# Six difference pieces of w_out: made in DRAM by an accumulating transfer, or on VectorE

## The chip, the core and the metric

The kernel runs on one core of one Trainium2 chip. The core has engines that each work through a queue of their own in order: TensorE (PE; its weight loads are shown as PEld), VectorE (DVE), ScalarE (ACT), GpSimd (POOL) and SyncE (SP), which issues the transfers of this kernel. The metric is the time of one execution on the device in microseconds (us).

## The reference

A gated linear attention runs over the sequence, and a feed-forward layer with squared ReLU follows. With batch 4, 8 heads, 768 steps and head size 48:

```python
for t in range(S):
    state = alpha[:, :, t, :, None] * state + np.einsum('bhd,bhe->bhde', k[:, :, t], v[:, :, t])
    y[:, :, t] = np.einsum('bhd,bhde->bhe', q[:, :, t], state)
x = y.transpose(0, 2, 1, 3).reshape(B * S, H * D)     # 3072 x 384
h = np.maximum(x @ w_in, 0.0)                         # w_in 384 x 2048
out = h * h @ w_out                                   # w_out 2048 x 384
```

All arrays are float32.

## The kernel before

The tokens are worked in 6 groups (`NG`) of 4 blocks (`GB`) of 128 tokens. For each group there are attention steps (states of blocks of 128 steps) and the two layers of the feed-forward part, `layer_in` (x times w_in) and `layer_out` (times w_out). The order of all work is written out by hand: a group's feed-forward steps are a list of `units`, each with a cost, and `weave` puts `events` (attention steps, loads, the preparation of weights) between them where the sum of the costs reaches the event's time. The events' times are numbers in the table `AT`; they are not microseconds. Each engine then runs its instructions in that order.

Group 0 and the first part of `layer_out` of groups 0 and 1 multiply in plain float32. Otherwise each float32 matrix is cut into two matrices of TensorE's faster type float32r, a high part and a rest, and a product is made of three passes. For weights, piece p of 8 (128 x 768 numbers, 384 KB) of layer w ("i" or "o") is prepared by four steps, `wstep` apart (`prepare`, line 580):

- `cast_w` (line 549): ScalarE writes the high part b, the tile `wb`. It stays in SBUF.
- `rest_w` (559): VectorE writes l = w - b, the tile `wl`.
- `scale_w` (563): ScalarE scales l by 1/E, and `keep` (555) has SP store it to DRAM.
- `diff_w` (568): VectorE writes d = b - l, the tile `wd`, and `keep` has SP store that, too.

VectorE's operations of these steps go through `combine` (line 545) and so all show line 547. Activations (x, h) are cut by `split_to` (595) and `diff_to` (599) in the same way.

The parts in DRAM are called `kept_parts`; in the profile `li`, `di`, `lo`, `do` are the l and d parts of w_in and w_out. `pump` (585) loads them back into `wl` and `wd` in the order of the list `todo`, when the part has been stored and the count of tiles in use allows it (`room`); `used` calls it when a part has been read for the last time in a group. All weights' tiles come from one pool of 26, `wt`. `stream` puts the parts of the next group on the list.

Of w_out, pieces 6 and 7 are prepared during group 0 (`o0`). Pieces 4, 5, 0, 1, 2, 3 are prepared during group 1, at the times 23, 26, 29, 35, 42, 36 (`o2`); `diff_w` stands 4.8 later. In group 1 the passes of `layer_out` (line 701, by `out_x` and `out_y`) read the parts of pieces 4 to 7, and pieces 0 to 3 are multiplied plainly by `out_plain`. The l parts of pieces 4 to 7 and the d parts of 6 and 7 stay in SBUF after their preparation; the d parts of pieces 0 to 5 don't, and are loaded from DRAM when they are wanted.

The attention of a pair of blocks is made of `turn` (transposes on TensorE of q and k, line 482, after the products of line 284 on VectorE), `ga` and `gb`. Between `ga` and `gb` a no-op on GpSimd hands over from matmuls of the one to those of the other:

```python
            passed = nc.gpsimd.nop(nofuse=True)
            dep(passed, end)
```

It waits for the last matmul of `ga`, and the first of `gb` waits for it. GpSimd has no other work after the kernel's first microseconds.

## Time and profile before

| what | value |
|---|---|
| median of 3 runs | 522.79 us (522.51 to 523.1) |
| span of the profiled execution | 520.6 us |
| PE busy | 510.8 us, 98% of the span |
| VectorE busy | 366.0 us, 70% |
| ScalarE busy | 313.0 us, 60% |
| GpSimd busy | 5.4 us, 1% |
| transfers | 102.36 MB, a mean of 197 GB/s; 68.3% of the 16 DMA engines' span |
| granted TensorE clock | 1.00 |

The profiled execution's own time is its span, from the first to the last instruction; the runs' times also hold what lies around the span, 2.2 us at the median. A line of a group in the profile reads: line, engine, operation, output<-inputs, shapes, count, then busy us, mean ns of one, and the idle time of the engine before them with what ended it. SPq is SP's queue of transfers. The stage in which the six pieces are prepared lies between about 165 and 205 us.

### The profile page before, as it was taken

How to read it: one execution, taken by the hardware profiler on the slowest of the kernel's cores; microseconds unless marked ns; L12 is line 12 of the kernel's file. 1: busy time of each engine (PE TensorE's matmuls, PEld its weight loads, DVE VectorE, ACT ScalarE, POOL GpSimd, SP SyncE). 2: the span in 40 equal slices, each digit the busy share in tenths (PEclk: the TensorE clock that was granted, in tenths of full speed). 3: DMA queues.
4: the chain of work that ended last, by engine and by line, in shares of the span. 5: the costliest groups of instructions: out<-in, count | busy, mean ns of one | idle time of the engine just before them, and what ended most of it. 6: DMA issues, size and time to landing. Idle time of an engine off the chain costs nothing.

```text
span 520.6 us, 12925 instructions
## 1 busy us (share of the span) xinstructions
PE 510.8 (98%) x5276; PEld 418.2 (80%) x5276; DVE 366.0 (70%) x631; ACT 313.0 (60%) x650; POOL 5.4 (1%) x29
## 2 busy tenths in 40 slices
PE   7989999999999999999999999999999999999997
PEld 4754455668887668988899988899988899988997
DVE  4798989979978787867597476587465476363861
ACT  4668785677888594575963275963275763164620
POOL 4000000000000000000000000000000000000000
PEclk9999999999999999999999999999999999999999
DMA  9999687244686787898884788964673534898201
GB/s 161 209 278 213 196 240 218 60 114 176 224 200 196 195 246 198 264 317 206 195 248 148 251 246 198 230 187 150 231 255 126 179 126 151 268 340 293 70 0 62
DMA packets 140995, 102.36 MB, mean 197 GB/s; under 512 B 111476, under 2 KB 114568, under 8 KB 140936
## 3 DMA queue, kind: packets, MB, share of 16 engines
q1 hardware_dynamic: 140936, 101.53, 68.3%
q8 instruction: 42, 0.69, 0.6%
q14 instruction: 17, 0.14, 0.1%
HBM read 84.18 MB, written 17.33 MB: 195 GB/s over the span
## 4 chain that ended last, share of the span: by engine, by line
PE 93%; DVE 2%; SPq 2%; DMA 1%; issue 1%; POOL 1%; ACT 0%; POOLq 0%; DVEq 0%
PE o L701 41%; PE h L622 32%; PE h L805 7%; PE y L352 4%; PE T L482 2%; PE sckv L372 2%; PE sckv L395 2%; PE cs L265 1%; DMA qk_lent<-in_q_dram 1%; SPq L303 1%; SPq L109 1%; PE cs L268 1%; PE cs L269 1%; DVE x L515 0%; DVE w_in L182 0%
## 5 line engine op out<-in xcount | busy, mean ns | idle before, releaser
L622 PE MATMUL h<-xa,wb 128*128 128x512 f32 x240 | 68.2, 392 | 0.0
L622 PE MATMUL h<-xl,wl 128*128 128x512 f32 x240 | 67.9, 391 | 0.0
L622 PE MATMUL h<-xd,wd 128*128 128x512 f32 x240 | 67.3, 396 | 0.0
L515 ACT COPY x<-y 32x256 f32<-32x256 f32 (+2 forms) x132 | 47.2, 366 | 25.4 <-PE y L352 20.1
L547 DVE TENSOR_TENSOR hid<-h,hid 128x512 f32<-128x512 f32 x40 | 27.6, 689 | 45.5 <-PE h L622 45.4
L701 PE MATMUL o<-wb,ha 128*128 128x384 f32 x160 | 54.6, 342 | 0.0
L701 PE MATMUL o<-w_out,hid 128*128 128x384 f32 x160 | 54.0, 491 | 0.0
L701 PE MATMUL o<-wd,hd 128*128 128x384 f32 x304 | 53.8, 334 | 0.0
L701 PE MATMUL o<-wl,hl 128*128 128x384 f32 x160 | 53.5, 335 | 0.0
L639 ACT ACTIVATE h<-h 128x512 f32<-128x512 f32 x40 | 23.3, 582 | 49.7 <-PE h L622 49.7
L622 PEld LDWEIGHTS h<-xl,wl 128*128 128x128 f32 x240 | 45.1, 188 | 10.0 <-DVE xl L547 0.4
L701 PEld LDWEIGHTS o<-wd,hd 128*128 128x128 f32 x304 | 52.7, 188 | 0.3 <-DVE osb L737 0.3
L622 PEld LDWEIGHTS h<-xa,wb 128*128 128x128 f32 x240 | 44.6, 188 | 9.3 <-ACT xa L596 0.2
L622 PEld LDWEIGHTS h<-xd,wd 128*128 128x128 f32 x240 | 44.2, 188 | 9.2
L701 PE MATMUL o<-wb,hx 128*128 128x384 f32 x144 | 48.7, 338 | 0.0
L701 PE MATMUL o<-wl,hx 128*128 128x384 f32 x144 | 48.1, 334 | 0.0
L701 PEld LDWEIGHTS o<-w_out,hid 128*128 128x128 f32 x160 | 29.8, 190 | 19.3
L637 ACT ACTIVATE hid<-h 128x512 f32<-128x512 f32 x40 | 24.0, 600 | 34.6 <-PE h L622 34.5
L805 PE MATMUL h<-x,w_in 128*128 128x512 f32 (+1 forms) x108 | 43.6, 552 | 1.2 <-ACT x L515 1.2
L596 ACT ACTIVATE ha<-hid 128x512 fp32r<-128x512 f32 x40 | 25.6, 639 | 25.5 <-DVE hx L547 16.1
L805 PEld LDWEIGHTS h<-x,w_in 128*128 128x128 f32 x108 | 19.9, 190 | 21.1 <-issue 17.2
L547 DVE TENSOR_TENSOR hl<-hid,ha 128x512 fp32r<-128x512 f32 x40 | 27.5, 688 | 10.1 <-ACT ha L596 10.1
(114 smaller groups left out, 879.7 us busy)
## 6 DMA issues: line engine op xcount, KB each, us to landing
wd<-do SPq DMA_DIRECT2D x36, 384.0 KB, 3.7
wl<-lo SPq DMA_DIRECT2D x34, 384.0 KB, 4.0
wl<-li SPq DMA_DIRECT2D x32, 384.0 KB, 3.5
wd<-di SPq DMA_DIRECT2D x32, 384.0 KB, 3.9
raw<-in_moe_w_in_dram SPq DMA_DIRECT2D x8, 768.0 KB, 5.6
raw<-in_moe_w_out_dram SPq DMA_DIRECT2D x8, 768.0 KB, 5.6
v_in<-in_v_dram SPq DMA_DIRECT2D x24, 192.0 KB, 4.7
out_dram<-osb SPq DMA_DIRECT2D x24, 192.0 KB, 1.9
```

Of the source, the lines that this page charges most:

```text
L352: ins = nc.tensor.matmul(out=ys[e][64 * half : 64 * half + D + G * e, m % 2, p // 2, t], lhsT=lhsT, rhs=rhs, start=(half, e) not in seen, ...
L372: nc.tensor.matmul(out=ps[e][HALF[h], 0, p, :], lhsT=ks[rows, p, HALF[h]], rhs=qs[rows, p, HALF[h]], start=True, stop=True, skip_group_che ...
L395: nc.tensor.matmul(out=ps[h][64 * e : 64 * (e + 1), 1, p, G:64], lhsT=tile_of("k", n)[HALF[h], 2 * p + e, :], rhs=tiles["v"][n % NV][HALF[ ...
L482: nc.tensor.transpose(out=ps[h][:, i, p, :], in_=rows[HALF[h], 128 * p : 128 * (p + 1)], identity=ident[HALF[h], HALF[h]],)
L515: copy(out=x[kk][to : to + m, t : t + 2], in_=blk[n]["y"][e][r : r + m, :, p // 2],)
L547: nc.vector.tensor_tensor(out=o, in0=x, in1=z, op=op)
L596: nc.scalar.activation(out=a, in_=x, func=AF.Copy, scale=NEAR)
L622: nc.tensor.matmul(out=acc["h", j], lhsT=here[w, "i", p][:, kk, jj * 128 : (jj + 1) * 128], rhs=x_parts[x][:, kk], start=start and kk == 0 ...
L637: nc.scalar.activation(out=hid[j], in_=x, func=AF.Copy, scale=E)
L639: nc.scalar.activation(out=x, in_=x, func=AF.Copy, scale=1.0 + E)
L701: nc.tensor.matmul(out=acc[t][:, 0:DM], lhsT=lhs[:, t * C : (t + 1) * C], rhs=rhs, start=start, stop=stop, skip_group_check=True,)
L805: nc.tensor.matmul(out=ps, lhsT=w[:, kk, c0 : c0 + 128], rhs=xT[g][kk][:, cols], start=(kk == 0), stop=(kk == KM - 1),)
```

## The change

For w_out's pieces 0 to 5 VectorE no longer makes d. `cast_w` has SP store the high part b at the place in DRAM where d is to be, and `diff_w` has GpSimd issue a transfer that adds the scaled rest l from SBUF to what lies there. So that an addition serves, the rest is scaled by -1/E instead of 1/E; the signs in `split_to` and `diff_to` are turned as well, so that the products of two rests are unchanged. For the other pieces VectorE adds instead of subtracting.

```diff
+    def summed(w, p):
+        return w == "o" and p < NW - AT["k0"]
+
     def cast_w(w, p):
         b = here["b", w, p] = wt("wb", FP32R, shapes[w])
         nc.scalar.activation(out=b, in_=whole[w][p], func=AF.Copy, scale=NEAR)
+        if summed(w, p):
+            nc.sync.dma_start(out=kept_parts["d", w, p], in_=words(b))
...
     def scale_w(w, p):
         l = made["l", w, p]
-        nc.scalar.activation(out=l, in_=l.bitcast(FP32), func=AF.Copy, scale=1.0 / E)
+        nc.scalar.activation(out=l, in_=l.bitcast(FP32), func=AF.Copy, scale=-1.0 / E)
         keep("l", w, p)
 
     def diff_w(w, p):
         b, l = here["b", w, p].bitcast(FP32), made["l", w, p].bitcast(FP32)
-        d = made["d", w, p] = wt("wd", FP32R, shapes[w])
         cut.add((w, p))
-        combine(((d, b, ALU.subtract, l),))
-        keep("d", w, p)
+        if summed(w, p):
+            nc.gpsimd.dma_start(out=kept_parts["d", w, p], in_=words(l), accum_op=ALU.add)
+            stored.add(("d", w, p))
+        else:
+            d = made["d", w, p] = wt("wd", FP32R, shapes[w])
+            combine(((d, b, ALU.add, l),))
+            keep("d", w, p)
         for x in "ld":
+            if x == "d" and summed(w, p):
+                continue
             t = made.pop((x, w, p))
...
     def split_to(a, l, x):
         nc.scalar.activation(out=a, in_=x, func=AF.Copy, scale=NEAR)
-        combine(((l, x, ALU.subtract, a.bitcast(FP32)),))
+        combine(((l, a.bitcast(FP32), ALU.subtract, x),))
 
     def diff_to(d, a, l):
         nc.vector.scalar_tensor_tensor(
-            out=d, in0=a.bitcast(FP32), scalar=-E, in1=l.bitcast(FP32), op0=ALU.mult, op1=ALU.add
+            out=d, in0=a.bitcast(FP32), scalar=-E, in1=l.bitcast(FP32), op0=ALU.mult, op1=ALU.subtract
         )
```

## The prediction

> **What bounds the kernel now.** I read the page's busy row and chain first, then the windows of the stage in which the six pieces are prepared, then the waits and timelines of that stage. In this text a piece is named by its number in w_out; the six are prepared in the order 4, 5, 0, 1, 3, 2, and their accumulating transfers are called A4, A5, A0, A1, A3, A2.

> ```profile
> PE 510.8 (98%) x5276; PEld 418.2 (80%) x5276; DVE 366.0 (70%) x631; ACT 313.0 (60%) x650; POOL 5.4 (1%) x29
> PE 93%; DVE 2%; SPq 2%; DMA 1%; issue 1%; POOL 1%; ACT 0%; POOLq 0%; DVEq 0%
> 166.00:217.00 51.00, 50.04 (x742) 39.38 (x741) 40.85 (x73) 33.03 (x76) 0.00 (x0) 1.00 0.76 210
> ```

> The first line is the busy time of each engine, the second the chain that ended last, the third the window 166 to 217 us (PE, PEld, DVE, ACT, POOL busy; granted clock; DMA share; GB/s). TensorE is busy for 50.04 of 51 us at full clock and makes the chain. VectorE is busy for 40.85, so it has 10 us to spare. The waits of this window and the timelines of PE, VectorE, ScalarE and SP give the few places where another engine comes close:

> ```profile
> PE y L352 <- issue: 1.0, 1, 1.0
> PEld T L482 <- DVE q_in L284: 0.5, 1, 0.5
> DVE wl L547 <- DMA do<-wd: 0.2, 1, 0.2
> ```
> ```profile
> 181.32 0.84 ACT L565 ACTIVATE wl<-wl 128x768 fp32r<-128x768 f32 x1
> ...
> 189.41 0.96 DVE L547 TENSOR_TENSOR wl<-w_out,wb 128x768 fp32r<-128x768 f32 x1 [0.19 <-DMA do<-wd]
> ...
> 191.89 0.96 DVE L547 TENSOR_TENSOR wd<-wb,wl 128x768 fp32r<-128x768 f32 x1
> 192.76 0.55 DVE L284 TENSOR_TENSOR q_in<-q_in,b 128x384 f32<-128x384 f32 x1
> ...
> 194.97 0.46 PE L482 MATMUL T<-ident,k_in 64*128 64x64 f32 x8
> 204.05 0.33 PE L352 MATMUL y<-am,v_in 64*48 64x64 f32 x3 [0.96 <-issue]
> 211.75 5.71 PE L701 MATMUL o<-wd,hd 128*128 128x384 f32 x32
> ```

> In the second fence the columns are start, duration, engine, line, operation. TensorE's only idle time in the stage is the 0.96 us before 204.05, which no engine ends. No wait of TensorE's matmuls is put down to a `wd` operation.

> **Removed.** Six VectorE subtractions of one 128x768 piece:

> ```profile
> L547 DVE TENSOR_TENSOR wd<-wb,wl 128x768 fp32r<-128x768 f32 x6 | 5.7, 954 | 0.4 <-PE o L701 0.4
> ```

> That is 6 x 0.954 = 5.7 us of VectorE, all beside TensorE's matmuls. The bound of the gain is TensorE's idle time in the stage, 0.96 us; I take 0, since that gap has no releaser on VectorE. The six stores of d behind `diff_w` go, too.

> **Added on SP.** Six stores of the high part, as many bytes as the six that go, but issued at `cast_w`. SP is in order, so each holds the queue until ScalarE's cast ends. Piece 4's cast ends at 165.8 and the `row` stores behind it, at 163.7 before, come some 2.5 us later; the `last` loads that read those rows are issued at 169.6, after loads that wait for the transposes of 167.7, and VectorE uses them first at 176.9. Covered. The stores of pieces 1 and 3 wait for casts that end near 188.4 and push two a_in loads from 187.5 to about 188.9; these belong to the next stage, which begins at 217. Covered. Without the cover a held SP costs its holding time.

> **Added on POOL.** Six accumulating transfers. POOL's queue else carries in this stage only the two hand-offs of line 456, at 176.86 and 204.42, for which TensorE waits at 179.52 and 207.31. In program order A4 stands before the first; A0, A1 and A3 before the second. A4 can start at 169.6 (end of its scaling), A3 at 193.0, so POOL's own time for issuing one would have to pass 9.9 us, or some 14 us, before TensorE waits. The trace has no transfer issued by POOL; an issue by SP is 0.32 to 0.47 us here. Cost 0.

> **The accumulate's duration, T.** No row shows one. [...] The nearest rows:

> ```profile
> wd<-do SPq DMA_DIRECT2D x36, 384.0 KB, 3.7
> ...
> lo<-wl SPq DMA_DIRECT2D x8, 384.0 KB, 2.6
> ```

> These are sizes and median us from issue to landing. Lower end: one plain store, 2.6. Upper end: a store and a load one after the other, each as slow as seen in this stage under load: the d store of 185.51 that held VectorE until 189.41, 3.9, and the longest load landing here, 5.6; together 9.5. I take 2.6 + 3.7 = 6.3, since an accumulate is a load and a store. [...]

> **Who waits for an accumulate.** In the changed program's order there are three kinds.
> First, SP's loads of d. The load of piece 4's d waits for A4: from 169.6 by T it goes out at 175.9, against 176.35 before, because there the store of d had to land first as well. It is first read at 211.75. Behind it on SP stand the store for piece 0, a store and loads of k and v; the k load, at 177.26 before, must be out by about 187 to land (4.3) before VectorE scales k at 191.34, so A4 could take 17 us. The load of piece 5's d, at 185.99 before, waits for A5, 176.9 + 6.3 = 183.2. Covered.
> Second, SP's loads into the tiles that A1, A3 and A2 read from (203.68, 205.39 and 219.18 before). If the transfers go one after another, A1 ends at 198.2, A3 at 204.5, A2 at 210.8. Covered, A3 by 0.9 on SP and by another 4 until TensorE needs piece 7 near 215.
> Third and closest, VectorE: the rest of piece 3 at 189.41 is written to the tile that A0 reads from. Before, this instruction waited 0.19 us for the store of d. Behind it in VectorE's queue are the four products of k and q, which TensorE transposes from 194.97. From 189.41 to the last product's end, 193.31, are 3.90 us; the `wd` that goes takes 0.87 of it, 3.03 are left, so A0 may land as late as 194.97 - 3.03 = 191.9 without TensorE waiting. A0 starts when piece 0 is scaled, 182.2, or after A5, 183.2: it lands at 189.5. No stall, 2.4 us to spare.

> **The sum.** The profiled execution has a span of 520.6 us; the median of the runs is 522.8, so 2.2 us lie outside the span and stay. 520.6 - 0 + 0 + 2.2 = 522.8.

> **Rival 1, slower: A0 lands late.** The mechanism is the third wait. If the transfers of POOL's queue go one after another, A0 lands at 169.6 + 3T and decides from T = 7.4; if they overlap, at 182.2 + T, from T = 9.7. For it: between 178 and 196 us the DMA share is 0.82 to 0.99, and T's range of 2.6 to 9.5 holds the point. Against: the rows' medians stay below it. Midway between 7.4 and 9.5, T = 8.45, A0 lands at 194.95, 3.0 us too late: 525.8. At 9.5 it is 198.1 and 6.2: 529.0. A slower T costs three times its excess.

> **Rival 2, slower: TensorE's instruction supply.** The gap of 0.96 us stands in a burst of small matmuls, released by nothing. The page lists 42 instruction packets (0.69 MB) that share the DMA engines. If they cause such gaps, more traffic causes more: one each in the bursts at 174 to 181 and 200 to 209, where accumulates are under way, is up to 3 x 0.96, so 523.8 to 525.7. Against: of the four bursts only one has a gap today.

> **Rival 3, faster.** The shifted traffic lets that gap go, and the shorter VectorE queue any wait hidden in the overlapped matmuls: the longest such wait in the waits view is 1.1 us (PEld y, issue), so 521.7. A larger gain would need TensorE to wait for VectorE inside its busy time. The stretch 181.07 to 189.08, 24 of `o<-w_out` without a gap, speaks against it. [...]

> **Rival 4: it doesn't do what it says.** The change could leave the work in place, if the dependence of A on the stored high part made POOL wait past the use. The program order has six VectorE operations fewer and the waits above, so 0.02; the time would be that of the sum.

> **How the numbers follow.** No change 0.42 (522.8, own range 521.8 to 523.8: a measurement of this kernel tells about 0.2%, 1.05 us, from no change), A0 late 0.30, instruction supply 0.14, faster 0.12, nothing done 0.02. Within 0.2% is 0.42 + 0.02 = 0.44, slower 0.30 + 0.14 = 0.44, faster 0.12. The likeliest single case is the sum. The range goes from rival 3's 521.7 to rival 1's upper end of T, 529.0; beyond lie a T over 9.5 and a gain over 1.1 us.

> **What would show it.** Right: PE busy near 50 of 51 us in 166 to 217; VectorE 5.7 us less there; the POOL transfers near 170, 177, 182, 192, 194 and 204; the rest of piece 3 starting before 191.9; transposes near 195. Rival 1: that instruction waits for a transfer of POOL's and "T <- DVE" shows the stall. Rival 2: "y <- issue" or "sckv <- issue" grows. Wrong: a T above 9.5, a POOL issue of over 9 us before a hand-off, or a difference outside the span.

## The result and the profile after

The changed kernel takes 528.52 us (median of 4 runs, 526.66 to 530.13) against 522.65 (4 runs, 522.49 to 523.1) before. The ratio is 1.0105, with a 95% interval of 1.0079 to 1.0131: 5.9 us slower. The profiled execution took 528.02 us with a span of 526.2, so 1.8 us lie outside the span. In the executions of the kernel before whose span is on record, 1.7 to 2.0 us lie outside it, so the difference is inside the span. (The 2.2 us of the prediction took a median of several runs and the span of one.)

The lines that answer to those of before: the busy row, the chain that ended last, and two rows of the table of DMA queues (packets, MB, share of 16 engines), all from the page of the changed kernel.

```profile
PE 512.9 (97%) x5276; PEld 419.7 (80%) x5276; DVE 360.2 (68%) x625; ACT 312.8 (59%) x650; POOL 10.7 (2%) x35
PE 91%; DMA 3%; SPq 2%; ACT 1%; issue 1%; DVE 1%; DVEq 0%
q0 software_dynamic: 864, 2.36, 2.8%
q8 instruction: 42, 0.69, 0.6%
```

VectorE has six operations fewer and 5.8 us less work, as announced. GpSimd has six more, 5.3 us together. The two last rows are the accumulates' packets, which are new, and the packets that carry instructions, which are as many as before. The chain's share of DMA, 3% against 1%, comes from the start-up: its two new long pieces there, 3.6 us from 24.51 and 5.3 us from 29.69, lie ahead of any accumulate. The window of the stage (changed kernel, same columns as before), and its waits on TensorE and GpSimd:

```profile
166.00:217.00 51.00, 47.37 (x715) 36.48 (x714) 31.25 (x60) 31.48 (x74) 5.34 (x6) 0.97 0.94 228
```
```profile
POOL do L577 <- DMA do<-wb: 22.2, 2, 12.7
PE y L352 <- issue: 3.6, 2, 2.0
PEld T L482 <- DVE q_in L284: 0.5, 1, 0.5
```

TensorE is busy for 47.37 us of 51 instead of 50.04, its clock is 0.97 instead of 1.00, and its waits for "issue" have grown from one of 1.0 us to two, 3.6 us together. The wait for VectorE is the same 0.5 as before. In the timeline of TensorE:

```profile
178.76 0.46 PE L352 MATMUL y<-am,v_in 64*48 64x64 f32 x15 [1.64 <-issue]
...
207.45 0.33 PE L352 MATMUL y<-am,v_in 64*48 64x64 f32 x3 [1.99 <-issue]
```

The first gap is new; the second is the gap that stood at 204.05 before (0.96 us), now twice as long. Behind the second the granted clock is 0.50 for 3.41 us, from 208.08 to 211.49. What follows is seen in windows of 3.4 us:

```profile
204.70:208.10 3.40, 1.41 (x54) 1.20 (x46) 1.57 (x6) 0.84 (x1) 0.00 (x0) 1.00 0.40 73
208.10:211.50 3.40, 3.40 (x13) 3.40 (x12) 0.31 (x1) 0.00 (x0) 0.86 (x1) 0.50 1.01 308
211.50:214.90 3.40, 3.40 (x107) 3.10 (x106) 0.96 (x3) 1.82 (x6) 0.00 (x0) 1.00 1.01 294
```

Of the first window TensorE idles for 1.99 us; through the next the granted clock is 0.50, and only 13 matmuls get done. They start 0.32 us apart instead of 0.173; the delay that this adds is about 1.5 us.

**Where the 5.9 us are.** TensorE issues the same instructions in the same order in both kernels, so the start of the n-th record (matmul or weight load) can be compared. The table gives how much later the profiled execution is than that of before, gained in four stretches:

| kernel | to record 3700 (176 us) | 3700 to 3900 (the gap at 178) | 4450 to 4600 (the gap at 204 to 207, clock) | last record |
|---|---|---|---|---|
| after | 0.54 | 1.86 | 2.57 | 4.92 |
| no_add | 0.05 | 0.31 | 0.18 | 0.81 |
| plain_pool | 0.04 | 0.00 | 0.76 | 0.76 |
| only_4 | 0.12 | 1.87 | 0.39 | 2.31 |
| only_1_3 | 0.35 | 0.00 | 0.18 | 0.49 |
| only_5_0_2 | -0.08 | 0.31 | 2.37 | 2.60 |
| a4_early | 0.56 | 0.86 | 0.19 | 1.55 |
| dve_back | 0.01 | 2.00 | 2.58 | 4.96 |

Of the changed kernel's 4.92 us, 4.43 arise in two places: 1.86 at the new gap, and 2.57 at the old one, of which some 1.0 is the longer gap (1.99 - 0.96) and 1.5 the clock. The first column is start-up, where executions of any of these kernels differ by as much as half a microsecond; the end of the span adds some 0.6.

**What the gaps are.** The trace has 42 instruction packets of 16 KB for TensorE's 10702 records (here its semaphore instructions are counted too), so one packet feeds a block of some 256. TensorE runs dry exactly at the records 3777 and 4545, three blocks of 256 apart, in every kernel here that has these gaps and leaves TensorE's instructions as they are. In the nineteen such gaps of all these traces (0.6 to 2.0 us) TensorE resumed 1.25 to 1.67 us after the packet that feeds it had ended (1.40 in the kernel before, 1.32 and 1.41 in the changed one). Before, the packet for block 3777 ran from 173.58 to 174.51, and the block was wanted at 176.34: 1.8 us ahead, no gap. Of these 1.8 us only an estimated 0.2 to 0.6 were to spare, by the 1.25 to 1.67 that TensorE took after the packet's end in the gaps. After, it starts at 176.50. The DMA view shows the packet of the kernel before, for 173.4 to 174.6 us, then what came ahead of it in the changed kernel, once for 172.4 to 176.4 us and once for 176.4 to 177.5:

```profile
q8 instruction: 1, 0.02, 4.8%
```
```profile
q0 software_dynamic: 144, 0.39, 63.8%
```
```profile
q8 instruction: 1, 0.02, 5.3%
```

The first accumulate's packets (from 172.49 to 176.23) took 63.8% of the DMA engines' time in that stretch, and no packet of q8 is among its rows (of q14 there is one, of 8 KB, from 175.19). The packet of block 3777 follows them directly, and 2.26 us after its start TensorE goes on, at 178.76. The packet for block 4545 starts at 204.59 (201.69 before), 1 us after the packets of the accumulates of pieces 1 and 3 have ended (197.09 to 203.62), and takes 1.44 us instead of 0.96. While it is on its way the engines are busy with SP's transfers; the view for 203.7 to 206.2 us has no row of the accumulates' queue:

```profile
q1 hardware_dynamic: 1769, 0.22, 70.6%
```

In none of the traces does a packet start earlier than 298 instructions before the block that it feeds (294 in the kernel before, 293 in the changed one). So in a burst, where 256 last some 2 us, no packet was early. The gap of the kernel before needs no other transfer: its DMA engines were busy for 0.03 of the time from 200.70 to 202.60 us, when the packet for block 4545 came, and TensorE still had to wait for it.

### The profile page after: what moved, and what is told of

It reads as the page before. It is cut to its first block, busy times and chain, and to the rows that moved or that the text cites. A ratio compares the mean times of both kernels' runs of the same rounds, so it can differ in the third digit from the quotient of the medians.

```text
span 526.2 us, 12932 instructions
## 1 busy us (share of the span) xinstructions
PE 512.9 (97%) x5276; PEld 419.7 (80%) x5276; DVE 360.2 (68%) x625; ACT 312.8 (59%) x650; POOL 10.7 (2%) x35
## 3 DMA queue, kind: packets, MB, share of 16 engines
HBM read 84.18 MB, written 19.69 MB: 197 GB/s over the span
## 4 chain that ended last, share of the span: by engine, by line
PE 91%; DMA 3%; SPq 2%; ACT 1%; issue 1%; DVE 1%; DVEq 0%
PE o L712 41%; PE h L633 31%; PE h L816 7%; PE y L352 4%; PE sckv L372 2%; PE T L482 2%; PE sckv L395 2%; DMA a_in<-in_alpha_dram 2%; PE cs L265 1%; DMA qk_lent<-in_q_dram 1%; SPq L303 1%; SPq L109 1%; DMA row<-b 1%; PE cs L268 1%; PE cs L269 1%
## 5 line engine op out<-in xcount | busy, mean ns | idle before, releaser
L547 DVE TENSOR_TENSOR hid<-h,hid 128x512 f32<-128x512 f32 x40 | 27.5, 688 | 45.5 <-PE h L633 45.5
L712 PE MATMUL o<-wl,hx 128*128 128x384 f32 x144 | 49.2, 341 | 0.0
L547 DVE TENSOR_TENSOR hl<-ha,hid 128x512 fp32r<-128x512 f32 x40 | 27.5, 687 | 10.9 <-ACT ha L607 10.9
## 6 DMA issues: line engine op xcount, KB each, us to landing
wd<-do SPq DMA_DIRECT2D x36, 384.0 KB, 4.5
wl<-lo SPq DMA_DIRECT2D x34, 384.0 KB, 4.3
wl<-li SPq DMA_DIRECT2D x32, 384.0 KB, 3.8
wd<-di SPq DMA_DIRECT2D x32, 384.0 KB, 3.9
```

The source lines that it names most:

```text
L547: nc.vector.tensor_tensor(out=o, in0=x, in1=z, op=op)
L712: nc.tensor.matmul(out=acc[t][:, 0:DM], lhsT=lhs[:, t * C : (t + 1) * C], rhs=rhs, start=start, stop=stop, skip_group_check=True,)
```

## The experiments

Theory S (instruction supply): the accumulates delay TensorE's instruction packets; in a burst of small matmuls a block of 256 instructions lasts only some 2 us (in the kernel before 1.8 ahead of record 3777, 2.1 ahead of 4545), so a late packet is a gap, and a long gap brings a low clock. Set against it: that the cost comes from VectorE's shorter queue and the changed order; from the earlier stores of the high part; from any transfer that GpSimd issues; or from a wait of SP's or VectorE's for an accumulate.

### no_add: the change without its transfers

The six accumulates are left out (so the d parts lack the rest); the removed subtractions, the earlier stores and the signs stay.

```diff
-            nc.gpsimd.dma_start(out=kept_parts["d", w, p], in_=words(l), accum_op=ALU.add)
```

> The changed kernel without its six accumulating transfers; the high parts are still stored early by SP, VectorE still makes no d (the d parts of pieces 0 to 5 in DRAM then hold only the high parts). Theory S (instruction supply: TensorE gets its instructions in blocks of 256 by a transfer of 16 KB each, and an accumulate in flight delays the block that a burst of small matmuls needs): the gap near 178 falls from 1.86 us to under 0.3, the gap near 205 returns to about 1.2, no drop of the clock, 522.0 to 522.9 us. Theory M (the moved stores of the high parts and SP's new waits do it): stays above 526.

Measured: 523.08 us (10 runs, 522.81 to 523.7), ratio 1.0008 [0.9999, 1.0017]. Its window:

```profile
166.00:217.00 51.00, 49.75 (x739) 38.94 (x738) 34.84 (x66) 33.08 (x76) 0.00 (x0) 1.00 0.75 211
```

The time is a little above the range that S gave. VectorE's work is down by 6.0 us and TensorE's busy time is 0.3 us under that of before. So the removal, the new order and the earlier stores together are worth between nothing and 0.9 us of loss; the transfers are the cost.

### plain_pool: the same transfers without the addition

```diff
-            nc.gpsimd.dma_start(out=kept_parts["d", w, p], in_=words(l), accum_op=ALU.add)
+            nc.gpsimd.dma_start(out=kept_parts["d", w, p], in_=words(l))
```

> The same six transfers issued by GpSimd, without the addition (the d parts of pieces 0 to 5 then hold only the scaled rest). Theory S: what counts is how long the packets hold the DMA engines; a 3072 B packet takes 0.12 us instead of 0.25, a transfer about half as long, the gap near 178 falls under 1.0 us, 522.5 to 526 us. Theory P (any transfer issued by GpSimd does it, by its own path): as the changed kernel, both gaps near 2 us, 526 to 530.

Measured: 524.88 us (7 runs, 523.86 to 528.49), ratio 1.0059 [1.0036, 1.0082]. There is no gap at 178, and the only one left in the stage's waits is that near 204:

```profile
PE y L352 <- issue: 1.7, 1, 1.7
```

By the medians 2.1 us of the 5.9 come with a plain transfer on this queue, the rest with the addition and the longer time that it takes; the profiled execution was the fastest of the seven, so the table shows only 0.76 of it. The packets differ by twice the time for the same bytes: one of 6144 B takes 0.234 us here, an accumulating one of 3072 B at least 0.252 and on average 0.31. The first plain transfer's packets end at 173.04, before the packet of block 3777 starts (173.16). So this run shows that a shorter transfer is out of the way in time, not that plain packets would leave an instruction packet alone.

### only_4, only_1_3, only_5_0_2: which of the transfers

```diff
     def summed(w, p):
-        return w == "o" and p < NW - AT["k0"]
+        return w == "o" and p in (4,)          # (1, 3) and (5, 0, 2) in the other two
```

> The change for piece 4 alone; VectorE makes the other five d. Theory S (a block of 256 TensorE instructions is held back by an accumulate in flight): piece 4's transfer runs at 171 to 175 us, when the block for the burst at 174 is asked for, so the gap near 178 is there (1.5 to 2 us) and the one near 205 is as before (1.2 to 1.4): 524 to 525 us. If the cost were spread evenly over the six, it is a sixth of it: 523.7 with no new gap.

> The change for pieces 1 and 3 alone, whose transfers run at 195 to 203 us. Theory S: no gap near 178; the gap near 205 is longer than before, 1.9 to 2.3 us instead of 1.2, and where it fills most of one 3.4 us window of the clock a stretch at half clock follows, in some of the executions: 523.3 to 526 us, with more scatter than before. Spread evenly: 524.6 with no change of the gap.

> The change for pieces 5, 0 and 2 alone, whose transfers run between the bursts (180 to 189, and behind 209 us). Theory S: blocks come later but are not yet needed; no new gap, no drop of the clock, 522.6 to 523.6 us. Spread evenly: 525.5.

Measured: 524.46 us [1.0012, 1.0054] with piece 4 alone, 523.68 [0.9995, 1.0036] with 1 and 3, 524.0 [1.0001, 1.004] with 5, 0 and 2 (10 runs each; before 522.77). The waits for issue in the stage of only_4, then of only_5_0_2:

```profile
PE y L352 <- issue: 3.0, 2, 1.6
```
```profile
PE y L352 <- issue: 1.8, 1, 1.8
```

Piece 4 alone makes the whole gap at 178 (1.87 us of delay in the table), and the others add no more than 0.31 there: its packets end at 175.34 and the instruction packet starts at 175.90. For the second gap the split is less clean. Pieces 1 and 3 alone, whose packets end at 200.62, leave the gap nearly as it was, 1.1 us, where S expected 1.9 to 2.3. Pieces 5, 0 and 2 lengthened it in the profiled execution to 1.8 us and brought the low clock, although their packets end at 189.55, 13 us ahead: that was not expected. Here are its windows, the second at half clock:

```profile
202.70:206.10 3.40, 1.62 (x47) 1.41 (x38) 3.08 (x7) 0.84 (x1) 0.06 (x1) 1.00 0.48 119
206.10:209.50 3.40, 3.40 (x13) 3.40 (x12) 0.00 (x0) 0.00 (x0) 0.80 (x1) 0.50 0.96 256
```

The three parts add up to 1.7 + 0.9 + 1.2 = 3.8 us, and the whole costs 5.9. That the rest comes from the second gap, which with all six is long enough for the low clock, fits but was not tried by itself. One drop of 3.4 us lowers a run's mean clock by 0.3%; it is 0.994 to 0.997 in three of the four runs of the changed kernel and 0.999 in the fourth, which at 526.66 us is still 4.0 slower than before.

### a4_early and moved: the same transfers at other times

a4_early prepares piece 4 three units earlier, moved also pieces 1 and 3 (the fourth and sixth entry). Each edit changes this one entry of the table `AT`:

```diff
-'o2': (23, 26, 29, 35, 42, 36)
+'o2': (20, 26, 29, 35, 42, 36)     # a4_early
+'o2': (20, 26, 29, 32, 42, 33)     # moved
```

> The changed kernel with one number of the table different: piece 4 is prepared 3 units earlier (o2 begins with 20 instead of 23), so that its accumulating transfer runs near 164 to 170 us and is over before the burst at 175. Theory S (instruction supply): the gap of 1.9 us near 178 goes (under 0.5 us), the gap near 205 and the drop of the clock behind it stay; some 2 us less than the changed kernel, 525 to 528 us. Theory P (anything on GpSimd's path) expects the gap near 178 to stay, since piece 5's transfer follows the hand-off as before: 526 to 530.

> As a4_early, and pieces 1 and 3 are prepared 3 units earlier too (o2 is 20, 26, 29, 32, 42, 33), so that all accumulating transfers but the last are over before the burst at 202 us. Theory S: both gaps return to those of the kernel before (none near 178, about 1.2 near 204), no drop of the clock, 522.5 to 524 us. If the transfers cost time in another way (more traffic for the loads, VectorE or SP waiting for them), it stays above 525.

Measured: a4_early 525.63 us (7 runs, 524.66 to 528.05), ratio 1.0057 [1.004, 1.0075]; moved 528.48 (4 runs, 527.45 to 530.49), 1.0105 [1.0082, 1.0128].

In a4_early the accumulate's packets end at 171.44, 4.8 us earlier; the instruction packet starts at 175.07 instead of 176.50, the gap at 178 goes from 1.64 to 0.63 us of idle, the second to 1.17, and the stage has no drop of the clock. S had expected the second gap and its drop to stay. So the time follows when piece 4's steps and its transfer run, with the same VectorE and the same amount of transfers. The first gap is not gone: the packet still starts 1.5 us later than before (0.6 of it from this execution's start-up), 3.6 us after the accumulate's last packet, so waiting for the accumulate to end is not all of the delay.

moved missed its expectation (522.5 to 524). The new times put preparation in front of the decay sums, and TensorE gets a wait that it did not have:

```profile
PE cs L268 <- DVE hi L256: 2.0, 2, 1.2
PE y L352 <- issue: 1.8, 2, 1.6
```

The first gap of supply has gone in this kernel, the second (1.65 us before 209.93) has not, and two drops of the clock follow, at 193.4 and 210.5. As a whole it tells little, only that the room for such shifts is small; but the second gap speaks against a simple S, since the accumulates' packets had ended at 201.80, 5.8 us before its packet starts.

### after_pad52, before_pad52, before_padlate: the blocks shifted

Thirteen tiny matmuls (26 more matmul and 26 more weight-load instructions in the page's busy row) move every later instruction of TensorE by 52 places in its blocks. after_pad52 and before_pad52 have them at the start, before_padlate (5 + 4 + 4) in group 0's first layer, at 31 to 36 us. Their results aren't used. The first edit is that of the two kernels with 52 in their name, the second that of before_padlate.

```diff
+        for _ in range(PADS.pop(0)):
+            nc.tensor.matmul(
+                out=ps[:, 0, 0:16], lhsT=s_t[3].rearrange("a p d -> a (p d)")[:, 0:128],
+                rhs=s_t[3][:, 0, 0:16], start=True, stop=True,
+            )
+
+    PADS = [4, 3, 3, 3]
```
```diff
-    def ffn_in(g, j, cols=slice(0, GB * C)):
+    def ffn_in(g, j, cols=slice(0, GB * C), pads=0):
...
+        for _ in range(pads):
+            nc.tensor.matmul(
+                out=ps[:, 0:16], lhsT=w[:, 0, 0:128], rhs=w[:, 0, 0:16], start=True, stop=True
+            )
...
-    steps["ha"] = lambda j: ffn_in(0, j, slice(0, HT))
-    steps["hb"] = lambda j: ffn_in(0, j, slice(HT, 2 * HT))
+    steps["ha"] = lambda j: ffn_in(0, j, slice(0, HT), 0 if j else 5)
+    steps["hb"] = lambda j: ffn_in(0, j, slice(HT, 2 * HT), 4)
```

> The changed kernel with 13 tiny matmuls (52 TensorE instructions) more in the warm-up of the first 25 us, so that every later block of 256 instructions ends 52 instructions earlier in the program; nothing else differs. Theory S: the blocks that the two bursts need are asked for before the bursts begin, several us earlier; both gaps fall under 0.7 us, the clock stays at 1.0, 522.3 to 524.5 us. Theories M and P: the transfers are unchanged, so the gaps and 526 to 530 us stay.

> The kernel before with the same 13 tiny matmuls in the warm-up. Theory S: the one gap of 1.18 us near 204 is a block that comes late as well and goes; no other block boundary falls so badly; 521.2 to 522.0 us. If the gap belongs to the place (the y matmuls and their data) and not to the block boundary, it stays near 204 and the time at 522.6 to 523.3.

> The kernel before with 13 tiny matmuls (52 TensorE instructions), this time between 31 and 36 us where TensorE waits for ScalarE, behind the burst that the earlier padding starved. Theory S: block boundaries from 40 us on are those of the padded kernel, the gap of 1.2 us near 204 goes, no drop near 35 us, less up to 0.8 us for a small gap near 246: 521.4 to 522.6 us, the fastest kernel so far. If the boundary is not the cause of the gap: 522.8 to 523.5.

Measured: after_pad52 527.14 us (4 runs), 1.01 [1.007, 1.0129]; before_pad52 524.28 (7 runs), 1.0034 [1.0023, 1.0046]; before_padlate 522.01 (12 runs, 521.88 to 522.79), 0.9981 [0.9964, 0.9998].

Both kernels with pads at the start missed what S had expected (522.3 to 524.5 and 521.2 to 522.0). The pads cost more than they bring, for a reason that fits S: they move another block's edge into the burst at 33 us, where a gap and half clock follow (0.50 from 35.1 to 38.5 us in before_pad52). In before_pad52's timeline:

```profile
33.24 0.37 PE L359 MATMUL y<-qs,us 48*64 48x64 f32 x10 [1.87 <-issue]
```

Between the two padded kernels, which share this, the change costs 527.14 - 524.28 = 2.9 us, half of the 5.9 without pads, with gaps of 0.80 and 0.6 us in the stage and no drop of the clock there. These two, and the gap at 33 us, stand at the records 4033, 4545 and 961 of the padded kernel: whole blocks of 256 from the gaps without pads, though other instructions stand there, shifted by 52 places. That the gaps belong to the blocks is shown by this better than by the times. before_padlate has an edge that matters neither in that burst nor in that of 204: in the stage's waits the entry of PE's `y` for issue is gone, and it is 0.76 us faster than the kernel before, near the length of the gap (0.96); the interval only just excludes no change. It has more work than the kernel before and is the fastest kernel of this study. Besides the 52 instructions, only where the blocks end was changed.

### dve_back: VectorE's work put back

Beside each accumulate VectorE writes d again, into a tile that nobody reads.

```diff
             nc.gpsimd.dma_start(out=kept_parts["d", w, p], in_=words(l), accum_op=ALU.add)
+            d = wt("wd", FP32R, shapes[w])
+            combine(((d, b, ALU.add, l),))
```

> The changed kernel with the six VectorE operations put back beside the accumulating transfers (their results are not stored). Theory S: VectorE was never on the path, so the time is that of the changed kernel, 526.5 to 530 us. If VectorE's 5.7 us had been worth something, it is slower than the changed kernel by up to that, 530 to 534.

Measured: 526.56 us (4 runs, 526.02 to 528.16), 1.006 [1.0043, 1.0077]; the profiled execution took 528.16. Its waits for issue in the stage:

```profile
PE y L352 <- issue: 3.8, 2, 2.0
```

The two gaps and the drop are those of the changed kernel, and the last record is as late (4.96 us against 4.92) with VectorE's work back. By the ratios it costs 3.4 us instead of 5.9, and the two intervals just miss each other; why it should be faster isn't known, and four runs of each, whose mean clock differs from run to run, are few. It isn't slower, so VectorE's time was worth nothing here.

### late_handoff: idle time alone, without accumulates

The kernel before, with idle times of growing length made by GpSimd ahead of the last six hand-offs, to see when the clock falls.

```diff
+    LATE = [0] * 6 + [18, 28, 22, 32, 26, 42]
...
+            for _ in range(LATE.pop(0)):
+                passed = nc.gpsimd.memset(causal, 0.0)
```

> The kernel before with GpSimd busy (18, 28, 22, 32, 26 and 42 fills of 128x128) ahead of the last six hand-offs between ga and gb, so that TensorE stands idle for some 0.3 to 4 us each, waiting and not for want of instructions. It measures the clock by itself: if a gap of TensorE lowers the granted clock, the longer gaps (over about 1.9 us) are each followed by a stretch near 3.4 us at half clock, and the shorter ones are not; 530 to 545 us. If the drop of the clock in the changed kernel had another cause, all gaps leave the clock at 1.0.

Measured (one run): 558.54 us, span 556.8, mean clock 0.972. The idle times came out longer than the 0.3 to 4 us that were meant, and so did the time. One of 2.05 us before 243.85 brings no drop (1.55 of it lie in one window), those of 3.10 before 271.41 and 3.09 before 331.00 bring one of 3.4 us, and those of 4.02 to 6.75 bring drops of 6.8 and 10.2. The windows around the first drop:

```profile
269.60:273.00 3.40, 1.59 (x97) 1.54 (x97) 3.05 (x5) 0.80 (x3) 1.41 (x7) 0.99 0.02 7
273.00:276.40 3.40, 3.40 (x13) 3.40 (x12) 1.96 (x6) 3.25 (x9) 0.00 (x0) 0.50 0.83 163
276.40:279.80 3.40, 3.40 (x21) 3.40 (x20) 2.92 (x5) 3.06 (x7) 0.00 (x0) 1.00 0.79 246
```

TensorE idled for 1.81 us of the window that precedes the drop, much as in the changed kernel (1.99) and in only_5_0_2 (1.78). So half clock came here without an accumulate, behind idle time alone. That it is set window by window, and that the idle time within one window counts, is the author's reading: in the changed kernel the clock goes to 0.50 at 208.08 and again at 525.52, behind the last work, and the 317.44 us between them are 93 times the 3.413 of the first drop. By windows counted back from 208.08 the changed kernel's first gap, 1.64 us, lies across an edge at 177.4 (1.40 of it behind the edge), and it brings no drop. The amount isn't sharp. In moved a window with 1.65 us idle (207.1 to 210.5) is followed by a drop, and in dve_back one with 1.76 us (176.6 to 180.0) is not; what else counts stays open. In most of these runs about half of a window was enough.

## Why the prediction was right and wrong

The forecast was 522.8 us and the result is 5.7 us over it, just below the upper end of the range. That end came from Rival 1, which did not happen, so the result lies in the range by luck.

**Right, the removal at nothing.** no_add has all of it and is at 1.0008 of before; dve_back puts it back and is no slower than the changed kernel.

**Right, T.** 6.3 us was taken, the rows of a load and a store added up (3.7 + 2.6). That an accumulate is made of these two no run shows: by the pages HBM was read for 84.18 MB in both kernels, and written for 19.69 MB after against 17.33 before. What the runs show is the time to landing. The DMA view of the changed kernel for 170 to 182 us and for the stage from 166 to 217 (KB each, median us from issue to landing):

```profile
do<-wl POOLq DMA_DIRECT2D x2, 384.0 KB, 6.3
```
```profile
do<-wl POOLq DMA_DIRECT2D x6, 384.0 KB, 6.5
```

The plain transfers of plain_pool took 4.4 us at the median.

**Right, POOL's issue.** It takes 0.86 to 1.01 us, against the 9.9 from which it would have counted. But POOL's queue had waits that the prediction did not list: A5 was issued at 179.89, not 176.9, since it stood behind the hand-off (8.4 us for `y`), and the two waits above, 22.2 us together, are for the stores of the high part. A1 and A3 went out at 195.23, not 192 and 194, and A2 at 209.78, not 204. SP's loads into the tiles that A1 and A3 read went out 4 us later than before. TensorE waited for none of that.

**Right, the three kinds of waits; Rival 1 did not happen.** The load of piece 4's d went out at 176.73 (forecast 175.9). A0 was issued at 184.86, before A5 had landed (186.15), but the packets of the two ran one after the other, from 181.82 to 185.81 and from 186.31 to 189.25. A0 took 4.8 us from issue to landing, so it ended where it was put (189.69 against 189.5), though A5 was issued 3 us later. The rest of piece 3 follows without a wait for it, in VectorE's timeline, and the products and the transposes behind it are in time:

```profile
190.61 2.03 DVE L547 TENSOR_TENSOR wl<-w_out,wb 128x768 fp32r<-128x768 f32 x2
192.80 0.56 DVE L284 TENSOR_TENSOR k_in<-k_in,inv 128x384 f32<-128x384 f32 x1 [0.16 <-ACT inv L280]
```

**Wrong, the step that failed: the sum had no term for what the added transfers do to the other queues of the DMA engines.** "520.6 - 0 + 0 + 2.2" counted only the transfers' own waiters. Rival 2 named the mechanism and had 0.14; its sign, that "y <- issue" grows, is the one that came (1.0 to 3.6 us). Its price was mis-sized twice: it took each gap at the 0.96 us seen, where the new one delays TensorE by 1.86 and the old one by another 1.0; and it had no price for the clock, 1.5 us. That makes some 4.4, against its 0.96 to 2.9.

What spoke against it, "of the four bursts only one has a gap today", was the weak step. It took no gap for no risk. The trace of before held the numbers that were needed: at the old gap TensorE resumed 1.40 us after its packet's end, and the packet for the burst at 174 to 181 ended 1.8 us before its block was wanted. That left some 0.4 us, and an accumulate of 6.3 us was to be issued just ahead. Each burst asks for its margin; it can't be read from the idle time.

**Still open.** Why the packet of block 3777 started only behind the first accumulate (176.50, after 176.23) isn't shown: the trace has each packet's start and time, but not what waits ahead of it in an engine. The second gap also changes by up to 1 us with transfers that are long over (only_5_0_2, moved) or plain (plain_pool), and what moves its packet by that is open. Loads of SP that run at another time are a candidate that was not tried. Of the changed kernel's 5.9 us, about 1.4 lie outside the two places: 0.5 at the start, 0.6 at the end of the span, and the rest between the profiled execution and the median. Four runs can't tell whether they belong to the change.

## What to carry to other kernels

Where TensorE is the bound and a stretch is made of many tiny matmuls, look up in the trace when the instruction packet for each such stretch lands and when it is wanted, before putting transfers ahead of it: here it landed 1.8 us ahead, TensorE took up to 1.67 in the gaps to go on after a packet's end, and an accumulate ahead of it made a gap. Moving work from an engine with time to spare to the DMA engines gained nothing here and cost time in what those engines carry besides; and a gap of 1.99 us in TensorE's work had half clock behind it for 3.41 us, another 1.5 us of delay. Thirteen useless matmuls in the right place took away the gap of the kernel before, so a gap that no engine ends is worth trying by shifting the instructions.
